# Attention scores of every block as float32 on 64x64 tiles of the matmul engine, two quads to a run

## The chip, the cores and the metric

The kernel runs on 1 core of one Trainium2 chip. The metric is the device time of one execution in microseconds (us), the median over runs.

## The reference

Sliding-window attention over 4 sequences of 576 tokens, 8 heads of 64 dimensions, window 64, and behind it two feed-forward networks without a residual path.

```python
scores = scale * np.matmul(q, k.transpose(0, 1, 3, 2))        # scale = 1/8
mask = (rel >= 0) & (rel < window)                            # rel = query - key
scores = np.where(mask, scores, -1000000000.0)
scores = scores - np.max(scores, axis=-1, keepdims=True)
attn = np.exp(scores)
attn = attn / (np.sum(attn, axis=-1, keepdims=True) + 1e-09)
return np.matmul(attn, v).astype(np.float32)
...
h = x @ w_in; r = np.maximum(h, 0.0); g = r * r               # first network, 512 -> 2048 -> 512
return (g @ w_out).astype(np.float32)
...
g = np.maximum(0.01 * h, h)                                   # second network, same sizes
```

x has 2304 rows (4 x 576) of 512 columns. The weights of both networks come as float64 and are turned into float32 on the chip.

## The kernel before, in words

**Blocks and quads.** The 2304 tokens are 18 blocks of 128 queries. A block has two quads (c = 0, 1) of four heads each. Within a block the queries are two halves (g = 0, 1) of 64, and each half sees 128 keys, its own 64 and the 64 before; a block's keys are 192 columns (KW).

**Token groups.** `BLOCKS` cuts the tokens into groups t of 512, 384, 512, 384, 512. The first network runs group by group, with 16 chunks of its 2048 hidden columns (`step`, lines 578 to 652): a chunk's 12 matmuls into bank h (line 590), ReLU, square and the split of the result on ACT and DVE, then the 12 matmuls of an earlier chunk into the four banks acc (line 636). Products of the networks are split: each float32 operand is a rounded part (type float32r) and its remainder, and three float32r matmuls stand for one product. While group t runs, attention makes the x of group t+1, so attention's matmuls stand between those of the first network until some 422 us. From 508 us on the second network runs alone (lines 820 and 909). The first group runs as 256-column halves while its weights are still being converted (DVE lines 317 to 329 and 284, ACT lines 314 and 281).

**A quad** (`quad`, lines 398 to 569) has these steps: load v; scores; mask (line 375, DVE); row maximum (507, DVE); four exponentials with row sums (510, ACT); reciprocal (516, 517) and normalising (520, DVE); four transposes (531, PE) into bank t; copy to pt (ACT); eight matmuls with v, the weighing (537, PE), into bank t; the result into x as rounded part (ACT, line 281) and remainder (DVE, line 284). The scores come in three ways:
- blocks 0 and 1 ("early") and blocks 2 to 5 ("plain", `NPLAIN=6`): q and k of both quads are loaded once for a block (`pair_load`, line 383), quad 0 on partitions 0 to 63 and quad 1 on 64 to 127. Eight float32 matmuls of 64 rows by 64 columns on 128 key columns (line 435) go into bank s (the second early quad into bank h). In the trace a float32 matmul of lines 435 and 537 is two records.
- blocks 6 to 17 (split): each quad loads q and k twice, onto both partition halves (line 459, 4 loads), ACT rounds k to kh and q to qs, DVE makes kl = k - kh and the remainder of q in the lower half of qs; eight matmuls of 128 rows by 128 columns on all 192 keys (line 485) in two groups of four, each group into bank s; each group is masked in two halves of 64 rows by 256.

Banks s and t and the SBUF tiles qr, qs, kr, kh, kl, u and pt are single buffers; v has two. Plain quads use u and kl in turn for the scores; split quads use u.

**The order of the work.** The program registers every operation with `op(engine, cost, due, fn, reads, writes)`: a cost and a due time, both written by hand. `Plan.order` (line 121) then plays the program through on the host: on each engine the ready operation with the earliest due time goes next, a slot is taken in the order of its registered turns, and a `margin` delays readiness. The order found there is fixed; on the chip each engine, and SP's queue of DMA issues, runs its list in order and waits where it must. `quads` gives every quad its time e, by which it should be done, evenly spread over the stretch in which its group must be made (`spread`, line 947). A split quad's scores are due at e - 8.0 and e - 7.2, its transposes at e - 1.6, its weighing at e - 0.4; a plain quad's scores at e - 6.5 f with f up to 1.3.

Of the kernel before, what the change touches and what calls it, by code (L numbers as in the profile page):

```python
# [41 lines left out]
    LAG=4, NPLAIN=6, NEARLY=2, SB=6, END=1.5, P0=5.2, LEAD=5.0, WF0=60.0, WF1=20.0, XC=18.0, WP=9.0, WO=8.0,  # L42
    AX=-1.0, AY=0.0, YP=1.0, FS=5.0, FMAX=1.3, EV0=0.5, EV1=1.5,
# [206 lines left out]
def build(ctx, tc, qp, kp, vp, w1, w2, caps, ident, out, prm=PRM):  # L250
# [147 lines left out]
    def quad(i, b, c, e, sp_):  # L398
        plain = b < prm["NPLAIN"]
        early = b < prm["NEARLY"]  # L400
        spare = 0.0 if plain else prm["SPARE"]
        f = min(max(sp_ / prm["FS"], 1.0), prm["FMAX"]) if plain else 1.0
        ax, ay = (0.0, prm["YP"]) if plain else (prm["AX"], prm["AY"])
        v = slot(wp, "w0", [P, 2, HQ * D], F32, NCH) if early else slot(vpool, "v", [P, 2, HQ * D], F32, 2)
        if early:
            u = slot(wp, "w1", [P, HQ, P], F32, NCH)
        elif plain and i % 2:
            u = slot(ap, "kl", [P, HQ, P])
        else:
            u = slot(ap, "u", [P, HQ, P])  # L410
        pt = slot(wp, "w0", [P, HQ, P], F32, NCH) if early else slot(ap, "pt", [P, HQ, P])
# [3 lines left out]
        if early:  # L415
            tp = slot(ps_acc, f"acc{i % 2 * 2}", [P, HQ, P])
            pv = slot(ps_acc, f"acc{i % 2 * 2 + 1}", [P, HQ // 2, P])
        else:
            tp = slot(ps_t, "t", [P, HQ, P])
            pv = slot(ps_t, "t", [P, HQ // 2, P])  # L420

        dma(
            e - min(9.0, 2 * sp_ - 0.6),
            lambda: nc.sync.dma_start(out=v.ap, in_=vp[b, c]), P * 2 * HQ * D * 4, writes=[(v, 0)],
        )
        if plain:
            q, k = pairs[b]
            st = slot(ps_h, "h", [P, HQ, P], F32, 2) if early and c else slot(ps_s, "s", [P, HQ, P])
            d = slice(c * D, (c + 1) * D)

            def scores():
                for h in range(HQ):
                    for g in range(2):
                        o = g * WIN
                        nc.tensor.matmul(
                            out=st.ap[o : o + WIN, h, :], lhsT=q.ap[d, h, o : o + WIN],
                            rhs=k.ap[d, h, o : o + P], start=True, stop=True,
                        )

            def mask():  # L440
                fst = (is_first(b, 0), is_first(b, 1))
                if fst[0] == fst[1]:
                    mask_into(u.ap, st.ap, slice(0, P), fst[0])
                else:
                    for g in range(2):
                        r = slice(g * WIN, (g + 1) * WIN)
                        mask_into(u.ap[r], st.ap[r], r, fst[g])

            op("pe", 1.1, e - 6.5 * f, scores, [(q, c), (k, c)], [(st, 0)])
            op("dve", dve_cost(512), e - 5.5 * f, mask, [(st, 0), cap], [(u, 0)])  # L450
        else:
            q = slot(ap, "qr", [P, HQ, P])
            k = slot(ap, "kr", [P, HQ, KW])
            qs = slot(ap, "qs", [P, HQ, P], F32R)
            kh = slot(ap, "kh", [P, HQ, KW], F32R)
            kl = slot(ap, "kl", [P, HQ, KW], F32R)

            def load(dst, src, g):
                nc.sync.dma_start(out=dst.ap[g * D : (g + 1) * D], in_=src[b, c])

            for g in range(2):
                dma(e + ax - 13.0, lambda g=g: load(q, qp, g), D * HQ * P * 4, writes=[(q, g)])
            for g in range(2):
                dma(e + ax - 12.9, lambda g=g: load(k, kp, g), D * HQ * KW * 4, writes=[(k, g)])
            op(
                "act", act_cost(HQ * KW), e + ax - 10.4, lambda: copy(kh.ap, k.ap),
                [(k, 0), (k, 1)], [(kh, 0)],
            )
            op(
                "dve", dve_cost(HQ * KW), e + ax - 10.0,  # L470
                lambda: sub(nc.vector, kl.ap, k.ap, kh.ap), [(k, 0), (k, 1), (kh, 0)], [(kl, 0)],
            )
            op("act", act_cost(512), e + ax - 10.0, lambda: copy(qs.ap, q.ap), [(q, 0), (q, 1)], [(qs, 0)])
            op(
                "dve", dve_cost(512), e + ax - 9.5,
                lambda: sub(nc.vector, qs.ap[D:P], q.ap[D:P], qs.ap[D:P]), [(q, 1)], [(qs, 0)],
            )
            for g in range(2):
                st = slot(ps_s, "s", [P, 2, 256])

                def scores(st=st, g=g):
                    for i2 in range(2):
                        h = 2 * g + i2
                        for m, kk in enumerate((kh, kl)):
                            nc.tensor.matmul(  # L485
                                out=st.ap[:, i2, 0:KW], lhsT=qs.ap[:, h, :], rhs=kk.ap[:, h, :],
                                start=m == 0, stop=m == 1,
                            )

                def mask(st=st, g=g, e2=0):  # L490
                    r = slice(e2 * WIN, (e2 + 1) * WIN)
                    mask_into(
                        u.ap[r, 2 * g : 2 * g + 2, :], st.ap[r, :, e2 * WIN : e2 * WIN + P],
                        r, is_first(b, e2),
                    )

                t0 = e + ax + 0.8 * g
                op("pe", 0.43, t0 - 7.0, scores, [(qs, 0), (kh, 0), (kl, 0)], [(st, 0)], margin=spare)
                for e2 in range(2):
                    op(  # L500
                        "dve", dve_cost(256), t0 - 6.2 + 0.3 * e2,
                        lambda m=mask, e2=e2: m(e2=e2), [(st, 0), cap], [(u, g, e2)],
                    )
        parts = [(u, 0)] if plain else [(u, g, e2) for g in range(2) for e2 in range(2)]
# [24 lines left out]
        def transpose():  # L529
# [3 lines left out]
        def weigh():  # L533
            for h in range(HQ):
                o = h % 2 * D
                for g in range(2):
                    nc.tensor.matmul(  # L537
                        out=pv.ap[o : o + D, h // 2, g * WIN : (g + 1) * WIN],
                        lhsT=v.ap[:, g, h * D : (h + 1) * D],
                        rhs=pt.ap[:, h, g * WIN : (g + 1) * WIN], start=True, stop=True,  # L540
                    )
# [21 lines left out]
        def part(m):  # L563
            return x.ap[:, m, kk, o : o + P]
# [512 lines left out]
```

## Time and profile before

| | us |
|---|---|
| median of 3 runs (884.1 to 886.19) | 885.02 |
| the profiled execution | 887.48 |
| its span, first to last instruction | 885.70 |
| PE busy in the span | 866.2 |
| DVE busy | 634.6 |
| ACT busy | 502.9 |

PE is the matmul engine, PEld its weight loads, which run beside the matmuls; DVE, ACT and POOL are the vector, scalar and general engines; SP issues the DMAs. A row names the line of the code, the engine, the operation and the tiles as out<-in. The starts of matmuls are measured; their ends are modelled, so busy times of neighbours overlap and a stretch is best measured from start to start. "x16" is the number of records in a merged row; a bracket at its end tells how long the engine stood idle before it and who ended that.

### The profile page before, as it was taken

How to read it: one execution, taken by the hardware profiler on the slowest of the kernel's cores; microseconds unless marked ns; L12 is line 12 of the kernel's file. 1: busy time of each engine (PE TensorE's matmuls, PEld its weight loads, DVE VectorE, ACT ScalarE, POOL GpSimd, SP SyncE). 2: the span in 40 equal slices, each digit the busy share in tenths (PEclk: the TensorE clock that was granted, in tenths of full speed). 3: DMA queues.
4: the chain of work that ended last, by engine and by line, in shares of the span. 5: the costliest groups of instructions: out<-in, count | busy, mean ns of one | idle time of the engine just before them, and what ended most of it. 6: DMA issues, size and time to landing. Idle time of an engine off the chain costs nothing.

```text
span 885.7 us, 13760 instructions
## 1 busy us (share of the span) xinstructions
PE 866.2 (98%) x5032; PEld 771.0 (87%) x5032; DVE 634.6 (72%) x1230; ACT 502.9 (57%) x1141; POOL 0.2 (0%) x4
## 2 busy tenths in 40 slices
PE   7789999999999999999999999999999999999998
PEld 6678788999888888999888899988899888999886
DVE  6989898777777787988666567695387775576540
ACT  5757776655454465655434366763377653567530
POOL 0000000000000000000000000000000000000000
PEclk8989999999999999999999999999999999999999
DMA  7665554324644436653534122331322422222201
GB/s 294 184 191 158 164 161 119 120 84 125 209 149 145 170 123 205 191 163 118 179 130 143 48 88 67 130 124 45 119 72 93 146 72 71 95 72 96 96 1 71
DMA packets 49795, 111.45 MB, mean 126 GB/s; under 512 B 6208, under 2 KB 7488, under 8 KB 49728
## 3 DMA queue, kind: packets, MB, share of 16 engines
q1 hardware_dynamic: 49728, 110.58, 39.0%
q8 instruction: 39, 0.64, 0.3%
q14 instruction: 28, 0.23, 0.1%
HBM read 92.73 MB, written 17.83 MB: 125 GB/s over the span
## 4 chain that ended last, share of the span: by engine, by line
PE 90%; DVE 5%; DMA 2%; ACT 2%; issue 1%; SPq 0%; DVEq 0%; ACTq 0%
PE h L590 21%; PE acc L636 20%; PE acc L909 15%; PE h L820 8%; PE s L820 6%; PE s L909 4%; PE t L909 4%; PE acc L820 3%; PE t L820 3%; PE s L485 2%; PE t L537 2%; PE t L531 1%; DMA wst<-w1b 1%; DVE u L375 1%; DMA wst<-w2a 1%
## 5 line engine op out<-in xcount | busy, mean ns | idle before, releaser
L590 PE MATMUL h<-x,w 128*128 128x512 f32 (+2 forms) x1008 | 225.5, 367 | 5.5 <-ACT e L610 2.7
L636 PE MATMUL acc<-g,w 128*128 128x512 f32 (+2 forms) x1008 | 222.6, 364 | 2.7 <-ACT g L281 2.7
L590 PEld LDWEIGHTS h<-x,w 128*128 128x128 f32 x1008 | 178.7, 191 | 28.4 <-ACT e L610 2.9
L636 PEld LDWEIGHTS acc<-g,w 128*128 128x128 f32 x1008 | 177.6, 191 | 23.9 <-ACT g L281 3.4
L909 PE MATMUL acc<-w,w 128*128 128x512 f32 x576 | 146.2, 389 | 0.0
L909 PEld LDWEIGHTS acc<-w,w 128*128 128x128 f32 x576 | 108.1, 188 | 22.4
L284 DVE TENSOR_TENSOR w<-wst,w 128x512 fp32r<-128x512 f32 (+1 forms) x144 | 87.2, 641 | 30.8 <-ACT w L281 30.8
L281 ACT CAST w<-wst 128x512 fp32r<-128x512 f32 (+1 forms) x144 | 78.8, 582 | 44.8 <-PE acc L909 25.2
L820 PE MATMUL h<-w,w 128*128 128x384 f32 x432 | 85.1, 334 | 0.0
L610 ACT ACTIVATE e<-h 128x512 f32<-128x512 f32 (+2 forms) x84 | 44.9, 534 | 60.8 <-PE h L590 60.2
L820 PEld LDWEIGHTS h<-w,w 128*128 128x128 f32 x432 | 75.9, 188 | 0.2
L314 ACT ACTIVATE wst<-wst 128x512 f32<-128x512 f32 x64 | 43.1, 674 | 49.4 <-DMA wst<-w1b 25.6
L375 DVE SCALAR_TENSOR_TENSOR u<-s,cap 64x256 f32<-64x256 f32 (+2 forms) x101 | 43.9, 434 | 21.0 <-PE s L485 18.0
L284 DVE TENSOR_TENSOR g<-e,g 128x512 fp32r<-128x512 f32 (+2 forms) x84 | 51.6, 614 | 8.9 <-ACT g L281 5.1
L820 PE MATMUL s<-w,w 128*128 128x384 f32 x288 | 57.9, 335 | 0.0
L619 DVE TENSOR_TENSOR e<-e 128x384 f32<-128x384 f32 (+1 forms) x64 | 39.7, 620 | 19.9 <-ACT g L618 19.6
L820 PEld LDWEIGHTS s<-w,w 128*128 128x128 f32 x288 | 50.7, 188 | 0.1
L510 ACT ACTIVATE u<-u,nm 128x128 f32<-128x128 f32 x112 | 43.6, 391 | 8.2 <-DVE nm L507 8.2
L323 DVE SCALAR_TENSOR_TENSOR e<-wst,e 128x512 int32<-128x512 int32 x64 | 44.2, 691 | 1.7
L329 DVE SCALAR_TENSOR_TENSOR e<-wst,e 128x512 int32<-128x512 int32 x64 | 44.1, 689 | 1.4
L281 ACT COPY pt<-t 128x512 f32<-128x512 f32 (+1 forms) x44 | 24.5, 556 | 36.2 <-PE t L531 31.4
L317 DVE TENSOR_SCALAR e<-wst 128x512 int32<-128x512 int32 x64 | 27.0, 421 | 20.3 <-ACT wst L314 19.3
(130 smaller groups left out, 1124.6 us busy)
## 6 DMA issues: line engine op xcount, KB each, us to landing
wst<-wf SPq DMA_DIRECT2D x96, 256.0 KB, 2.9
kr<-kp SPq DMA_DIRECT2D x48, 192.0 KB, 3.3
wst<-w1a SPq DMA_DIRECT2D x16, 512.0 KB, 3.8
wst<-w2a SPq DMA_DIRECT2D x16, 512.0 KB, 4.0
v<-vp SPq DMA_DIRECT2D x32, 256.0 KB, 2.9
wst<-w1b SPq DMA_DIRECT2D x16, 512.0 KB, 4.5
wf<-e SPq DMA_DIRECT2D x32, 256.0 KB, 2.4
wst<-w2b SPq DMA_DIRECT2D x16, 512.0 KB, 4.6
```

Source lines behind the costliest of these rows:

```text
L281: nc.scalar.copy(out=dst, in_=src)
L284: eng.tensor_tensor(out=lo, in0=src, in1=f32(hi), op=ALU.subtract)
L314: nc.scalar.activation(out=top, in_=top, func=AF.Copy, scale=2.0**-112)
L323: nc.vector.scalar_tensor_tensor(out=cv.ap, in0=words(1), scalar=-(1 << 31), in1=cv.ap, op0=ALU.bitwise_and, op1=ALU.bitwise_or,)
L329: nc.vector.scalar_tensor_tensor(out=cv.ap, in0=words(0), scalar=29, in1=cv.ap, op0=ALU.logical_shift_right, op1=ALU.bitwise_or,)
L375: nc.vector.scalar_tensor_tensor(out=u, in0=st, scalar=SCALE, in1=cap_s.ap[r, first, :].unsqueeze(1).to_broadcast([r.stop - r.start, st.sh ...
L510: nc.scalar.activation(out=u.ap[:, h, :], in_=u.ap[:, h, :], func=AF.Exp, bias=nm.ap[:, h : h + 1], scale=1.0, accum_out=sm.ap[:, h : h + 1],)
L590: nc.tensor.matmul(out=hp.ap[:, c0 : c0 + n1], lhsT=wi[:, a, kk, :], rhs=x.ap[:, b, kk, c0 : c0 + n1], start=(kk == 0 and m == 0), stop=(k ...
L610: nc.scalar.activation(out=r.ap, in_=hp.ap[:, c], func=AF.Relu)
L636: nc.tensor.matmul(out=ac[d].ap[:, c0 : c0 + n1], lhsT=wo[:, a, d * P : (d + 1) * P], rhs=g.ap[:, b, c0 : c0 + n1], start=begin, stop=end, ...
L820: nc.tensor.matmul(out=ps.ap, lhsT=view(v, i), rhs=xs[s, i][b].ap[:, u], start=begin and i == 0 and m == 0, stop=i == 1 and m == 2, skip_g ...
L909: nc.tensor.matmul(out=accs[3 * h + tt].ap, lhsT=v.ap[:, b, tt * P : (tt + 1) * P], rhs=w.ap[:, a, :], start=n == 0 and m == 0, stop=last ...
```

## The change

Blocks 0 to 3 keep `quad`, all of them with float32 scores; their tiles are u and pt in turn, and the transposed weights are copied back into the same tile. Blocks 4 to 17 (`NDUO=4`) become a `duo`: q and k of the block are loaded once; 16 float32 matmuls score both quads in one run, head by head, quad 0 into bank s and quad 1 into bank t; each quad is masked at once, quad 1 first; the two softmax chains follow, 2.2 us apart by their due times, quad 0 in u and quad 1 in pt; each quad is transposed into bank t and copied back; 16 matmuls weigh both in one run into one full bank t; one ACT copy and one DVE subtraction of 512 columns put the result into x. The scores are due at e - 12 (`DS`), the transposes at e - 5.2 and e - 3.4, the weighing at e - 1.8, with e that of the block's second quad. The split of q and k (lines 452 to 503) is gone. The planner's cost of an exponential is 0.57 us (`EXPC`) where it was 0.385, that of a score run 0.55 for a quad (1.1 before) and for a duo; the weighing of a duo has 1.1. `softmax` and `mask` hold the old steps unchanged; `load_v` is the old load.

```diff
--- before.py
+++ after.py
@@ -39,8 +39,8 @@
 NP = NCH // 2
 
 PRM = dict(
-    LAG=4, NPLAIN=6, NEARLY=2, SB=6, END=1.5, P0=5.2, LEAD=5.0, WF0=60.0, WF1=20.0, XC=18.0, WP=9.0, WO=8.0,
-    AX=-1.0, AY=0.0, YP=1.0, FS=5.0, FMAX=1.3, EV0=0.5, EV1=1.5,
+    LAG=4, NDUO=4, NEARLY=2, DS=12.0, EXPC=0.57, SB=6, END=1.5, P0=5.2, LEAD=5.0, WF0=60.0, WF1=20.0, XC=18.0, WP=9.0, WO=8.0,
+    YP=1.0, FS=5.0, FMAX=1.3, EV0=0.5, EV1=1.5,
     SPARE=0.2, NACT=0, WARM=20, WC=0.3, WD=1e6, AL=0.6, CS=0.7,
     QB=-0.5, QE=-2, QL=0.0, QT=1,
...
+    def scores(b, sts):
+
+        q, k = pairs[b]
+        for h in range(HQ):
+            for c, st in sts:
+                d = slice(c * D, (c + 1) * D)
+                for g in range(2):
+                    o = g * WIN
+                    nc.tensor.matmul(
+                        out=st.ap[o : o + WIN, h, :], lhsT=q.ap[d, h, o : o + WIN],
+                        rhs=k.ap[d, h, o : o + P], start=True, stop=True,
+                    )
...
+    def transpose(u, tp, pt, due):
+        def run():
+            for h in range(HQ):
+                nc.tensor.transpose(out=tp.ap[:, h, :], in_=u.ap[:, h, :], identity=id_s.ap)
+
+        op("pe", 0.44, due, run, [*((u, "n", h) for h in range(HQ)), idt], [(tp, 0)], margin=prm["SPARE"])
+        op("act", act_cost(512), due + 0.4, lambda: copy(pt.ap, tp.ap), [(tp, 0)], [(pt, "t")])
...
+    def weigh(v, pt, pv, k0):
+        for h in range(HQ):
+            o = h % 2 * D
+            for g in range(2):
+                nc.tensor.matmul(
+                    out=pv.ap[o : o + D, k0 + h // 2, g * WIN : (g + 1) * WIN],
+                    lhsT=v.ap[:, g, h * D : (h + 1) * D],
+                    rhs=pt.ap[:, h, g * WIN : (g + 1) * WIN], start=True, stop=True,
...
+    def to_x(b, pv, k0, k1, due):
...
+        n = (k1 - k0) * P
+        op("act", act_cost(n), due, lambda: copy(part(0), pv.ap), [(pv, 0)], hi)
+        op("dve", dve_cost(n), due + 0.3, lambda: sub(nc.vector, part(1), pv.ap, part(0)), [(pv, 0), *hi], lo)
...
+        u = slot(wp, "w1", [P, HQ, P], F32, NCH) if early else slot(ap, ("u", "pt")[i % 2], [P, HQ, P])
...
+        q, k = pairs[b]
+        st = slot(ps_h, "h", [P, HQ, P], F32, 2) if early and c else slot(ps_s, "s", [P, HQ, P])
+        op("pe", 0.55, e - 6.5 * f, lambda: scores(b, [(c, st)]), [(q, c), (k, c)], [(st, 0)])
+        op("dve", dve_cost(512), e - 5.5 * f, lambda: mask(b, u, st), [(st, 0), cap], [(u, 0)])
+        softmax(u, i < prm["NACT"], (e - 4.7 * f, e - 4.0 * f, e - 2.4 * f))
+        transpose(u, tp, u, e + ay - 1.6)
+        op("pe", 0.65, e + ay - 0.4, lambda: weigh(v, u, pv, 0), [(u, "t"), (v, 0)], [(pv, 0)])
...
+    def duo(b, e):
+
+        vs = [load_v(b, c, False, e - 12.0) for c in range(2)]
+        us = [slot(ap, ("u", "pt")[c], [P, HQ, P]) for c in range(2)]
+        sts = [slot(ps_s, "s", [P, HQ, P]), slot(ps_t, "t", [P, HQ, P])]
+        q, k = pairs[b]
+        op(
+            "pe", 0.55, e - prm["DS"], lambda: scores(b, list(enumerate(sts))),
+            [(q, 0), (q, 1), (k, 0), (k, 1)], [(st, 0) for st in sts], margin=prm["SPARE"],
         )
...
+        for c in (1, 0):
             op(
...
+                "dve", dve_cost(512), e - prm["DS"] + 1.0 + 0.1 * (1 - c),
+                lambda c=c: mask(b, us[c], sts[c]), [(sts[c], 0), cap], [(us[c], 0)],
+            )
+        for c in range(2):
+            d = 2.2 * c
+            softmax(us[c], False, (e - 9.8 + d, e - 9.0 + d, e - 6.4 + d))
+        for c in range(2):
+            transpose(us[c], slot(ps_t, "t", [P, HQ, P]), us[c], e - 5.2 + 1.8 * c)
+        pv = slot(ps_t, "t", [P, KD, P])
+
+        def run():
+            for c in range(2):
+                weigh(vs[c], us[c], pv, c * HQ // 2)
+
+        rd = [x for c in range(2) for x in ((us[c], "t"), (vs[c], 0))]
+        op("pe", 1.1, e - 1.8, run, rd, [(pv, 0)], margin=prm["SPARE"])
+        to_x(b, pv, 0, KD, e - 0.6)
...
@@ -973,14 +954,18 @@
     dma(-99.9, lambda: nc.sync.dma_start(out=cap_s.ap, in_=caps), P * 2 * P * 4, writes=[cap])
     dma(-99.8, lambda: nc.sync.dma_start(out=id_s.ap, in_=ident), P * P * 4, writes=[idt])
     pair_load(1, -99.0)
-    for b in range(2, prm["NPLAIN"]):
+    for b in range(2, NQB):
         e, _, _, gap = next(q for q in quads if q[1] == b)
-        pair_load(b, e - 6.5 * min(max(gap / prm["FS"], 1.0), prm["FMAX"]) - 6.0)
+        early = 6.5 * min(max(gap / prm["FS"], 1.0), prm["FMAX"])
+        pair_load(b, e - early - 6.0 if b < prm["NDUO"] else e + gap - prm["DS"] - 6.0)
     for k in range(2 * NCH):
         st = next(q for q in steps if q[2][0][2] == k // 2)
         weight(k, st[3] + (k % 2) * st[4] - prm["LEAD"])
     for i, (e, b, c, gap) in enumerate(quads):
-        quad(i, b, c, e, gap)
+        if b < prm["NDUO"]:
+            quad(i, b, c, e, gap)
+        elif c:
+            duo(b, e)
     for n, (t, i, parts, T, dt, wave) in enumerate(steps):
         last = n + 1 == len(steps) or steps[n + 1][0] != t
         T2 = steps[n + 1][3] + steps[n + 1][4] if n + 1 < len(steps) else t_end
```

## Rows read from the trace of the kernel before

**Rows 1.** The page's first part: each engine's busy time and share.
```profile
PE 866.2 (98%) x5032; PEld 771.0 (87%) x5032; DVE 634.6 (72%) x1230; ACT 502.9 (57%) x1141; POOL 0.2 (0%) x4
```

**Rows 2.** Table by stretches: length, busy PE, PEld, DVE, ACT, POOL, clock, DMA, GB/s.
```profile
24.00:68.00 44.00, 35.34 (x309) 31.79 (x304) 38.13 (x78) 30.00 (x91) 0.00 (x0) 0.88 0.61 188
...
121.00:425.00 304.00, 302.04 (x1939) 271.32 (x1939) 242.00 (x466) 171.78 (x435) 0.00 (x0) 1.00 0.48 148
...
508.00:885.70 377.70, 373.68 (x1884) 339.13 (x1882) 233.71 (x468) 210.83 (x418) 0.00 (x0) 1.00 0.26 86
```

**Rows 3.** Timeline of PE: start, us, engine, line, op, tiles; split scores.
```profile
321.79 2.88 PE L590 MATMUL h<-x,w 128*128 128x512 f32 x12
324.51 0.25 PE L485 MATMUL s<-kh,qs 128*128 128x192 f32 x1
...
324.93 1.56 PE L636 MATMUL acc<-g,w 128*128 128x512 f32 x6
326.33 0.25 PE L485 MATMUL s<-kh,qs 128*128 128x192 f32 x1
```

**Rows 4.** Timeline of PE: transposes, weighing and float32 scores of block 5.
```profile
100.71 0.60 PE L531 MATMUL t<-ident,u 128*128 128x128 f32 x4
101.06 1.63 PE L590 MATMUL h<-x,w 128*128 128x512 f32 x6
102.62 0.73 PE L537 MATMUL t<-pt,v 128*64 128x64 f32 x16
103.29 1.67 PE L590 MATMUL h<-x,w 128*128 128x512 f32 x6
104.80 2.91 PE L636 MATMUL acc<-g,w 128*128 128x512 f32 x12
107.63 1.09 PE L435 MATMUL s<-kh,qs 64*64 64x128 f32 x16
108.65 3.06 PE L590 MATMUL h<-x,w 128*128 128x512 f32 x12
111.55 0.62 PE L636 MATMUL acc<-g,w 128*128 128x512 f32 x2
```

**Rows 5.** Groups by line: a split score; one line: durations min/median/max of weighing.
```profile
L485 PE MATMUL s<-kh,qs 128*128 128x192 f32 x96 | 23.9, 275 | 0.5 <-DVE u L375 0.5
...
L537 PE MATMUL t<-pt,v x512: 222/222/271, 34.1 to 421.7; 128*64 128x64 f32 x171
```

**Rows 6.** Timeline of PE: two float32 quads back to back, banks s and h.
```profile
8.41 0.76 PE L435 MATMUL s<-w,w 64*64 64x128 f32 x10 [0.99 <-DVE w L375]
8.91 0.33 PE L435 MATMUL h<-w,w 64*64 64x128 f32 x2
9.00 0.28 PE L435 MATMUL s<-w,w 64*64 64x128 f32 x2
9.07 0.28 PE L435 MATMUL h<-w,w 64*64 64x128 f32 x2
9.11 0.28 PE L435 MATMUL s<-w,w 64*64 64x128 f32 x2
...
9.93 0.38 PE L967 MATMUL t<-w 128*128 128x128 f32 x1
```

**Rows 7.** Waits of PE from 68 to 508 us: total, times, longest.
```profile
PE t L531 <- DVE u L520: 0.6, 1, 0.6
PE s L485 <- DVE u L375: 0.5, 2, 0.3
```

**Rows 8.** Groups by line: the subtraction that makes kl, count, busy, mean ns.
```profile
L284 DVE TENSOR_TENSOR kl<-kr,kh 128x768 fp32r<-128x768 f32 x24 | 22.8, 950 | 0.6 <-PE t L531 0.6
```

**Rows 9.** SP's timeline, the chain that ended last, PE's timeline, near 55 us.
```profile
52.88 1.18 SPq L459 DMA_DIRECT2D qr<-qp  x2
...
55.45 5.53 DMA wst<-w2a
...
61.98 1.79 PE L590 MATMUL h<-x,w 128*128 128x256 f32 x9 [2.66 <-ACT e L610]
```

More of the change, by code (lines that the diff above doesn't have):

```diff
@@ L396, in pair_load, with mask, softmax @@
         dma(due + 0.01, lambda: load(k, kp), P * HQ * KW * 4, writes=[(k, 0), (k, 1)])
[L398 to L408, printed above, removed]
-        else:
-            u = slot(ap, "u", [P, HQ, P])
-        pt = slot(wp, "w0", [P, HQ, P], F32, NCH) if early else slot(ap, "pt", [P, HQ, P])
+    def scores(b, sts):
[9 more added lines that the diff above has]
+                    )
+    def mask(b, u, st):
+        fst = (is_first(b, 0), is_first(b, 1))
+        if fst[0] == fst[1]:
+            mask_into(u.ap, st.ap, slice(0, P), fst[0])
+        else:
+            for g in range(2):
+                r = slice(g * WIN, (g + 1) * WIN)
+                mask_into(u.ap[r], st.ap[r], r, fst[g])
+    def softmax(u, act_norm, due):
         nm = slot(sp, "nm", [P, HQ], F32, 3)
@@ L414, in quad @@
         rc = slot(sp, "rc", [P, HQ], F32, 3)
[L415 to L503, printed above, removed]
@@ L504, in quad @@
-        parts = [(u, 0)] if plain else [(u, g, e2) for g in range(2) for e2 in range(2)]
         def reduce_max():
@@ L527, in norm_head @@
             )
-        def transpose():
+        op("dve", dve_cost(512), due[0], reduce_max, [(u, 0)], [(nm, 0)])
+        for h in range(HQ):
+            op("act", prm["EXPC"], due[1], lambda h=h: exp(h), [(nm, 0), (u, 0)], [(u, "x", h), (sm, h)])
+        ex = [(u, "x", h) for h in range(HQ)]
+        op("dve", 0.25, due[2], recip, [(sm, h) for h in range(HQ)], [(rc, 0)])
+        if act_norm:
+            for h in range(HQ):
+                op("act", 0.2, due[2] + 0.2, lambda h=h: norm_head(h), [(rc, 0), (u, "x", h)], [(u, "n", h)])
+        else:
+            op("dve", dve_cost(512), due[2] + 0.2, norm, [(rc, 0), *ex], [(u, "n", h) for h in range(HQ)])
@@ L560, in quad @@
         o = b * P - starts[t]
[L561 removed]
         def part(m):
[L564 to L569 removed]
+            return x.ap[:, m, k0:k1, o : o + P]
@@ new lines, in to_x, with load_v @@
+        hi = [(x, 0, kk, b) for kk in range(k0, k1)]
+        lo = [(x, 1, kk, b) for kk in range(k0, k1)]
+        n = (k1 - k0) * P
+        op("act", act_cost(n), due, lambda: copy(part(0), pv.ap), [(pv, 0)], hi)
+        op("dve", dve_cost(n), due + 0.3, lambda: sub(nc.vector, part(1), pv.ap, part(0)), [(pv, 0), *hi], lo)
+    def load_v(b, c, early, due):
+        v = slot(wp, "w0", [P, 2, HQ * D], F32, NCH) if early else slot(vpool, "v", [P, 2, HQ * D], F32, 2)
+        dma(
+            due, lambda: nc.sync.dma_start(out=v.ap, in_=vp[b, c]), P * 2 * HQ * D * 4, writes=[(v, 0)],
+        )
+        return v
```

42 lines of the change are left out of this document (16 added, 26 removed).

## The prediction

> **What bounds the kernel now.** I read the page's busy line first: the matmul engine (PE) is busy for 98% of the span [rows 1]. That only says where to look, so the table by stretches came next [rows 2]. There the reader is to see three things. From 121 to 425 us, where blocks 6 to 17 are scored and weighed, PE is busy 302.04 of 304.00 us at a granted clock of 1.00, and DVE 242 of 304: PE's own work sets the time there, and DVE and ACT work that goes is worth only the waits that it ends. From 24 to 68 us PE is idle for 44.00 - 35.34 = 8.7 us, its clock is 0.88, and DVE is busy 38.13 of 44 us: there the work on weights and attention holds PE up. From 508 us on no attention is left; nothing of the change reaches that stretch except by its start.
>
> So the change is priced as PE time between fixed neighbours. In the timeline of PE, an instruction group's price is the start of the next group less its own start. Twelve undisturbed 512-column matmuls take 324.51 - 321.79 = 2.72 us, six 1.36 [rows 3]; what a neighbour takes above this is the price of going into or out of the group beside it.
>
> **PE, old pieces.** From rows 3 and 4:
> - one group of 4 split scores: 324.93 - 324.51 = 0.42, and the six matmuls behind it 326.33 - 324.93 = 1.40, so 0.04 on leaving: 0.46. A quad has two: 0.92. The 96 records of L485 with kh [rows 5] and as many with kl are 24 quads of 8, blocks 6 to 17;
> - four transposes: 0.35;
> - the six matmuls between transposes and weighing: 1.56, so 0.20 (I put half to each);
> - 8 weighing matmuls (16 records): 0.67 with rounding, taken as 0.66; leaving: 1.51 - 1.36 = 0.15;
> - 8 float32 64x64 scores of one quad (16 records): 1.02; entering 2.83 - 2.72 = 0.11, leaving 2.90 - 2.72 = 0.18: 1.31.
>
> Transposes and weighing together are 0.35 + 0.20 + 0.66 + 0.15 = 1.36 a quad. A block of two quads costs 2 x (0.92 + 1.36) = 4.56 with split scores, and 2 x (1.31 + 1.36) = 5.34 for blocks 4 and 5, which are float32 already but quad by quad.
>
> **PE, the new scores.** A duo's 16 matmuls are 32 records. The trace has no such run, but it has the nearest thing: in the first blocks the float32 scores of quad 0 (into bank s, contraction rows 0 to 63) and of quad 1 (into bank h, rows 64 to 127) stand back to back [rows 6]. The reader is to see that while both are there, 2 records of s and 2 of h start every 0.11 us (9.00, 9.07, 9.11), where s alone starts 2 in that time (16 in 1.02 us is 0.11 a pair, with the ends). The two row halves run side by side and neither slows the other. The duo alternates the halves head by head, into s and t, so its lower end is 8 steps of 0.11 with the same ends: 1.02 for both quads. The upper end is no overlap, twice the run: 2.04. Between lies the order of rows 6, all of one quad first: 9.93 - 8.41 = 1.52. I take 1.02, since alternating heads feeds both halves from the start; with 0.11 and 0.18 that is 1.31 a block. The Trainium skill ("TensorE: Matmul & The Clock Gate", Part 3, The mechanism) says that matmuls start and end strictly in program order. The trace differs: h's first two records start at 8.91, before s's last at 9.00 and later, although s stands first in the program. By that rule the duo would need one step of 0.11 more, some 1.5 us over 14 blocks.
>
> **PE, the new weighing.** One run of 32 records. In the old run of 16 the starts span 0.73 - 0.22 (one record [rows 5]) = 0.51, 0.034 a step; 16 more add 0.54: 0.66 + 0.54 = 1.20, with one entry (0.10) and one exit (0.15) 1.45. Upper end: 2 x 0.66 + 0.25 = 1.57.
>
> **Sum on PE.** New block: 1.31 + 2 x (0.35 + 0.10) + 1.45 = 3.66. Blocks 6 to 17: 12 x (4.56 - 3.66) = 10.8. Blocks 4 and 5: 2 x (5.34 - 3.66) = 3.4. Together **14.2 us** off the bound. Blocks 0 to 3 keep their PE work.
>
> **Waits of PE after 68 us.** They are few: 304.00 - 302.04 = 2.0 us up to 425 us [rows 2]. The 0.5 us of split scores that waited for the mask to free bank s goes, as a duo has two banks. The transposes' 0.6 us behind the normalising stays [rows 7].
>
> **Off PE, costed at nothing.** Per split quad go an ACT copy of k and of q, two DVE subtractions (the one of k 0.95 us [rows 8]) and four half-size masks, for which one full mask comes (two where only one half block is first of its sequence); a block's two x copies become one each on ACT and DVE. PE, busy 99% there, hides all of it; uncovered it could only gain. On SP a split quad's 4 loads of q and k become 2 a block. The copy of the transposes into u instead of pt adds no instruction. What it adds is a wait: the next block's masks need the weighing of this block done, and v's two buffers are both held by one duo, so SP's wait for them stands ahead of weight loads. Block spacing by the due times is 16 to 29 us against DS=12, so I price these waits at nothing, upper end in the rivals.
>
> **The stretch from 24 to 68 us.** PE's chain stands on a weight load that lands after 5.53 us, and PE idles 2.66 us for it; SP issued it behind the four q and k loads of block 6, the first of them at 52.88 us, right after block 4's scores had freed their tile [rows 9]. These become 2 loads, and stand behind a later scoring (block 4's duo is due 0.4 us after e of its first quad, not 8.4 before). Block 4's DVE work moves later too, out of a stretch where DVE is 87% busy. Bounds: worse by as much again (-2.7) to all 8.7 us of idle time gone. I take the 2.7 us of this one wait, the nearest row.
>
> **The forecast.** 14.2 + 0.5 + 2.7 = 17.4 us. The profiled execution took 887.5 us (885.7 span and 1.8 around it), so 870.1; the median of the runs is 885.0, 2.5 below it, so **867.6**.
>
> **Rivals.**
> 1. *The row halves don't run side by side* in this order. Scores 2.04: a block costs 4.68, so twelve lose 0.12 each (1.4) and two gain 0.66 each (1.3), nothing on PE; with the two smaller terms 885.0 - 3.2 + 0.1 = 881.9. Against it: rows 6. The Trainium skill (the same page, Part 2, Back-to-back issue gap) gives some 81 ns for each load and matmul of 128 columns in a sustained stream; an estimate by it is 32 x 0.081 = 2.6 us of scores a block, which would make the kernel some 5 us slower than before. The trace doesn't agree: 16 in 1.02 us are 64 ns, and half of that where two quads overlap. Chance 0.05.
> 2. *SP's queue blocks the weights.* The two v loads and the pair load of a duo wait for a weighing or a scoring that the planner believes done, and a weight load behind them comes late, as in rows 9, once or twice more: 2 x 2.7 lost, not 2.7 won, 885.0 - 14.7 + 5.4 = 875.7. For: that is how the present stall arose. Against: fewer loads than before. Chance 0.08.
> 3. *PE waits for the duo's chain* (slower). Place: bank t holds scores, two transposes and the result one after the other, and u is mask, weights and transpose in one; between scoring and weighing lie the masks, eight exponentials, normalising and two copies. If the planner has it end too early, PE stands before the transposes and again before the weighing. From 14.7 / 14 = 1.05 us of waiting a block on it decides; at 2 us a block it is 28 us: 885.0 - 14.7 + 28 = 898.3. For: scores are entered at 0.55 us and take 1.31. Against: PE itself is late by that, so what waits behind it in order is late too, and the exponentials are entered at 0.57, not 0.385. In the old chain PE waited 0.6 us once. Chance 0.05.
> 4. *The matmuls are not what the diff says* and nothing moves: 885. The 64*64 form is in the trace [rows 4], so 0.02.
>
> **The numbers.** Forecast 0.80. Low end: 14.2 + 0.5 + 8.7 gives 861.6. High end of the forecast's own terms: scores at 1.52 (14 x 0.50 = 7.0) and weighing at its upper end (1.7), no early gain: 885.0 - 14.7 + 8.7 = 879.0. The range 862 to 879 holds rival 2 as well; rivals 1, 3 and 4 and some tails lie outside. A measurement can tell about 0.2%, 1.8 us, from no change: faster is the forecast, rival 2 and most of rival 1 (0.91), same 0.04, slower 0.05.
>
> **What would show it.** The timeline of a duo: 32 score records of s and t mixed, some 1.0 us to the next group (rival 1: 2.0), and 32 weighing records in 1.2 us. PE's wait list after 68 us: still 2 us or less, with no transposes behind normalising or weighing behind a copy beyond 0.1 us a block (rival 3). The stretch to 68 us: PE idle 6 us, and no weight load landing after 5 us behind q and k (rival 2). The end of the first network's last matmul, 508 us now, some 17 us sooner, and from there on the same 378 us. The prediction fails if PE's idle time grows over the sum, or if that last stretch changes by more than 1 us.

## The result, and the profile after

The changed kernel took 872.37 us (median of four runs, one of which, of 4784.8 us, was disturbed and is left out of the ratio) where the kernel before, on the same chip, took 885.05: a ratio of 0.985 with an interval of 0.983 to 0.987. The forecast was 867.6 with a range of 862 to 879. Two repeats gave 0.983 (0.982 to 0.985) and 0.985 (0.983 to 0.988). The profiled executions stand further apart than the medians: 887.48 and 871.45, spans 885.70 and 869.66, so 16.0 us.

The page's first part, after; it answers to [rows 1]:

```profile
PE 849.9 (98%) x5224; PEld 755.1 (87%) x5224; DVE 574.8 (66%) x1100; ACT 469.5 (54%) x1079; POOL 0.2 (0%) x4
```

PE lost 16.3 us of busy time, the span 16.0. DVE lost 59.8 and ACT 33.4, and PE is as full as before: 98%. Its idle time in the whole span is 19.8 us where it was 19.5, so what was won is PE's own work. That is how it looks when one engine's work sets the time and its neighbours only follow.

The table by stretches, after, in the columns of [rows 2]:

```profile
24.00:68.00 44.00, 33.56 (x339) 30.37 (x339) 40.33 (x82) 32.71 (x92) 0.00 (x0) 0.92 0.57 195
...
121.00:425.00 304.00, 303.12 (x2165) 269.67 (x2165) 193.77 (x356) 147.26 (x392) 0.00 (x0) 1.00 0.39 131
```

From 121 to 425 us PE is idle for 0.9 us where it was 2.0. DVE's load there fell from 242 to 194 us, and PE ran at clock 1.00 both times. In the first stretch PE was to become less idle. It is idle for 44.00 - 33.56 = 10.4 us where it was 8.7, and DVE is busier (40.33, before 38.13).

The waits of PE from 68 to 508 us are now one; they answer to [rows 7]:

```profile
PE h L571 <- DVE w L284: 0.8, 1, 0.8
```

No transpose waits for a normalising and no weighing for a copy: from 68 us on the duo's chain never holds PE up.

The timeline of PE through one duo, after (start, us, engine, line, operation, tiles; a merged row ends with its number of records):

```profile
95.73 2.88 PE L617 MATMUL acc<-g,w 128*128 128x512 f32 x12
98.54 0.33 PE L406 MATMUL s<-kh,qs 64*64 64x128 f32 x2
98.55 0.33 PE L406 MATMUL t<-kh,qs 64*64 64x128 f32 x2
98.70 0.28 PE L406 MATMUL s<-kh,qs 64*64 64x128 f32 x2
98.71 0.28 PE L406 MATMUL t<-kh,qs 64*64 64x128 f32 x2
98.81 0.28 PE L406 MATMUL s<-kh,qs 64*64 64x128 f32 x2
98.82 0.28 PE L406 MATMUL t<-kh,qs 64*64 64x128 f32 x2
...
99.57 3.06 PE L571 MATMUL h<-x,w 128*128 128x512 f32 x12
102.47 2.88 PE L617 MATMUL acc<-g,w 128*128 128x512 f32 x12
105.19 2.88 PE L571 MATMUL h<-x,w 128*128 128x512 f32 x12
107.91 0.60 PE L463 MATMUL t<-ident,u 128*128 128x128 f32 x4
108.27 3.00 PE L617 MATMUL acc<-g,w 128*128 128x512 f32 x12
111.10 0.60 PE L463 MATMUL t<-ident,pt 128*128 128x128 f32 x4
111.45 2.33 PE L571 MATMUL h<-x,w 128*128 128x512 f32 x9
113.72 0.73 PE L472 MATMUL t<-u,v 128*64 128x64 f32 x16
114.23 0.69 PE L472 MATMUL t<-pt,v 128*64 128x64 f32 x16
114.85 0.98 PE L571 MATMUL h<-x,w 128*128 128x512 f32 x3
```

Read starts, not durations. The scores take 99.57 - 98.54 = 1.03 us for both quads; one quad alone took 1.02 [rows 4]. From 98.70 on, two records of s and two of t start every 0.11 us, each pair of t 0.01 us behind its pair of s. Entering costs 98.54 - 95.73 - 2.72 = 0.09 and leaving 102.47 - 99.57 - 2.72 = 0.18. The weighing takes 114.85 - 113.72 = 1.13. All 13 score runs from here on take 1.03. Block 4's, at 59.79 us, took 1.47: its records of t began 0.44 us behind those of s.

**A ledger of PE.** Take the stretch from the 97th matmul of the first network's first product (where the 512-column groups begin) to the first matmul of the second network, and add up every attention group from its start to the next group's start. Network matmuls are set at 226.7, 173.4 and 120.0 ns each by width, as they run undisturbed; what they take above that is "borders and waits".

| us | before | after |
|---|---|---|
| the stretch | 437.05 | 421.56 |
| network matmuls | 371.29 | 371.29 |
| scores | 23.93 | 13.44 |
| transposes | 9.98 | 9.99 |
| weighing | 18.89 | 15.81 |
| borders and waits | 12.96 | 11.04 |

Scores before were 48 split groups (21.89) and block 5's two float32 quads (2.04); after they are 13 runs. The stretch gives 15.5 us: 10.5 from scores, 3.1 from weighing, 1.9 from borders and waits. What lies outside it hardly moved. The second network to the end took 377.89 and 377.92 us. The stretch began at 70.76 before and at 70.18 after: 0.6 us.

### The profile page after: what moved, and what is told of

Read it like the earlier page. It is cut to its first block, busy times and chain, and to the rows that moved or that the text cites. A ratio compares the mean times of both kernels' runs of the same rounds, so it can differ in the third digit from the quotient of the medians.

```text
span 869.7 us, 13819 instructions
## 1 busy us (share of the span) xinstructions
PE 849.9 (98%) x5224; PEld 755.1 (87%) x5224; DVE 574.8 (66%) x1100; ACT 469.5 (54%) x1079; POOL 0.2 (0%) x4
## 4 chain that ended last, share of the span: by engine, by line
PE 92%; DVE 4%; DMA 2%; ACT 2%; issue 0%; DVEq 0%; SPq 0%
PE acc L617 21%; PE h L571 21%; PE acc L890 15%; PE h L801 9%; PE s L801 6%; PE s L890 4%; PE t L890 4%; PE acc L801 3%; PE t L801 3%; PE t L472 2%; PE s L406 2%; PE t L463 2%; DMA wst<-w2a 1%; PE t L948 1%; DVE e L323 1%; DMA wst<-w1a 1%
## 5 line engine op out<-in xcount | busy, mean ns | idle before, releaser
L571 PE MATMUL h<-x,w 128*128 128x512 f32 (+2 forms) x1008 | 219.3, 363 | 3.5 <-DVE w L284 1.9
L640 DVE COPY e<-acc 128x512 f32<-128x512 f32 (+1 forms) x19 | 12.6, 664 | 49.3 <-PE acc L890 27.8
L890 PE MATMUL s<-w,w 128*128 128x512 f32 x144 | 40.5, 389 | 0.0
L890 PE MATMUL t<-w,w 128*128 128x512 f32 x144 | 40.4, 389 | 0.0
L284 DVE TENSOR_TENSOR w<-x,w 128x384 fp32r<-128x384 f32 x54 | 29.5, 553 | 13.9 <-ACT w L281 13.9
```

What stands on the lines that cost most here:

```text
L284: eng.tensor_tensor(out=lo, in0=src, in1=f32(hi), op=ALU.subtract)
L571: nc.tensor.matmul(out=hp.ap[:, c0 : c0 + n1], lhsT=wi[:, a, kk, :], rhs=x.ap[:, b, kk, c0 : c0 + n1], start=(kk == 0 and m == 0), stop=(k ...
L890: nc.tensor.matmul(out=accs[3 * h + tt].ap, lhsT=v.ap[:, b, tt * P : (tt + 1) * P], rhs=w.ap[:, a, :], start=n == 0 and m == 0, stop=last ...
```

## The experiments

The texts on record call the theories by letters. In short: by **A** the gain is PE's own list, priced from start to start (in the first two texts A says something else, that single executions spread and mostly before 70 us); by **E** a part of it comes from the work that DVE, ACT and the DMAs lost; by **G** the loads of q and k hold up weight loads in the early stretch; by **I** the planner's new costs move the early start. The kernel before ran beside every experiment, the changed kernel beside some of them; where it didn't, a difference of two medians is one between chips, and the ledger's stretch, which repeats within 0.6 us, tells more.

### Both kernels again

Nothing is edited.

> The kernel before again, nothing edited, for a second trace of it. Theory A (the spread lies in the first 70 us): 884 to 886 us as timed, and the stretch from the 97th matmul of the first network to the start of the second takes 437.1 us as in the first trace, within 0.5. Theory B (it lies elsewhere): that stretch is shorter by 2 us or more.

> The changed kernel again, nothing edited. The two profiled executions differ by 16.0 us (887.5 and 871.5), the medians by 12.7. Theory A: the difference is the spread of single executions, most of it made before 70 us (the 26 warm-up records at the start took 4.84 us in one trace and 5.92 in the other). Then the median is 871 to 874 us, 11 to 14 us under the kernel before, and in a second trace the stretch from the 97th matmul of the first network to the start of the second again differs from the old trace by 15.5 us within 0.5. Theory B: the PE saving itself varies from run to run. Then that stretch moves by 2 us or more.

> The changed kernel once more, nothing edited, beside the next one on the same chip: 871 to 872.5 us, 0.983 to 0.985 of the kernel before, in its third trace the same weight load behind block 5's q and k after 5.4 us and PE idle 10 us from 24 to 68 us.

Before: 886.08 us, stretch 436.52. After: 871.18 and 871.94, stretches 421.23 and 421.35. So the ledger's stretch repeats within 0.6 us, and the two kernels differ there by 15.0 to 15.8 us in every pairing of the traces. The medians differ by 15.1 us (871.18 against 886.29 beside it) and 13.1 (871.94 against 885.02), where 12.7 came the first time; 11 to 14 had been expected. The place where it begins doesn't repeat: 70.76 and 70.04 before, 70.18, 70.02 and 70.93 after. The early gain of 0.6 us is within that. Single runs of the kernel before went from 883.7 to 890.5 (35 runs on one chip), so a difference of some 2 us between two single executions tells nothing.

### One quad after the other in the run

```diff
-        for h in range(HQ):
-            for c, st in sts:
-                d = slice(c * D, (c + 1) * D)
+        for c, st in sts:
+            d = slice(c * D, (c + 1) * D)
+            for h in range(HQ):
```

The same 16 matmuls, in another order; nothing else differs on any engine.

> The changed kernel with one edit: within a duo's score run all eight matmuls of quad 0 come before all eight of quad 1, where they alternated head by head. PE's list differs in that alone, the other engines' lists not at all. Theory A (the two row halves overlap as far as the order lets them): the run takes some 1.5 us to the next group in place of 1.03, as the early quads showed, so 14 x 0.49 = 6.9 us more than the changed kernel, 879 us. Theory C (the halves always run side by side, whatever the order): no change, 872. Theory D (the order does not matter because they share the bus and the gain has another cause): 872 with the run at 1.03.

It took 878.05, 6.9 more than the changed kernel beside it; 0.991 (0.989 to 0.993) of the kernel before. The timeline of PE:

```profile
98.54 0.76 PE L406 MATMUL s<-kh,qs 64*64 64x128 f32 x10
99.04 0.33 PE L406 MATMUL t<-kh,qs 64*64 64x128 f32 x2
99.14 0.28 PE L406 MATMUL s<-kh,qs 64*64 64x128 f32 x2
99.20 0.28 PE L406 MATMUL t<-kh,qs 64*64 64x128 f32 x2
...
99.42 0.71 PE L406 MATMUL t<-kh,qs 64*64 64x128 f32 x10
100.06 0.74 PE L571 MATMUL h<-x,w 128*128 128x512 f32 x2
```

Here s runs alone at first, then both, then t alone: 100.06 - 98.54 = 1.52, the pattern and the price of [rows 6]. Thirteen runs are 19.77 us, 6.3 more, and the stretch is 428.03, 6.8 more. So 6.3 of the 10.5 us that the scores gain hang on the order of two loops: with alternating heads both row halves of the array work from the first record to the last.

The prediction set a rule of the Trainium skill ("TensorE: Matmul & The Clock Gate", Part 3, The mechanism) against the trace: matmuls start strictly in program order. This run differs from it as the kernel before did, for all of s stands ahead of t in the program, and t's first pair starts at 99.04, before the pairs of s at 99.14 and later. Nor does the estimate of 2.6 us hold that the prediction worked out from the same page of the Trainium skill, Part 2 (Back-to-back issue gap): the run costs 1.03 with the halves alternating and 1.52 without.

### All blocks float32, quad by quad

```diff
-    LAG=4, NPLAIN=6, NEARLY=2, SB=6, END=1.5, P0=5.2, LEAD=5.0, WF0=60.0, WF1=20.0, XC=18.0, WP=9.0, WO=8.0,
+    LAG=4, NPLAIN=18, NEARLY=2, SB=6, END=1.5, P0=5.2, LEAD=5.0, WF0=60.0, WF1=20.0, XC=18.0, WP=9.0, WO=8.0,
```

This is the kernel before without its split: DVE, ACT and the DMAs lose what they lose in the change, but the quads stay apart.

> The kernel before with float32 64x64 scores for all 18 blocks (NPLAIN=18), quad by quad and weighed quad by quad: no split of q and k, but no joint runs. DVE, ACT and the DMA queue lose the same work as in the changed kernel. Theory A (PE's time between neighbours decides): 12 blocks cost 5.34 in place of 4.56 us, so 9.4 us slower than before, 894 us, 1 or 2 us less if waits on DVE go. Theory E (the gain of the change is the work that left DVE, ACT and SP): faster than before, 875 to 883.

It took 889.74, 1.004 (1.002 to 1.005) of the kernel before: slower, with DVE at 579.9 us (changed kernel 574.8) and ACT at 471.1 (469.5). The page's first part of this kernel:

```profile
PE 871.6 (98%) x5224; PEld 767.6 (87%) x5224; DVE 579.9 (65%) x1114; ACT 471.1 (53%) x1093; POOL 0.2 (0%) x4
```

PE's busy time rose from 866.2 [rows 1] to 871.6. E falls, for nearly all the relief of DVE and ACT is here, the kernel is no faster, and in the ledger borders and waits didn't shrink (13.63, before 12.96). A had the sign and missed the size: 3.4 us where 9.4 were expected; the ledger's stretch, 440.74, is 3.7 longer. Its timeline of PE shows why:

```profile
209.87 1.09 PE L435 MATMUL s<-kr,qr 64*64 64x128 f32 x16
210.89 0.66 PE L531 MATMUL t<-ident,kl 128*128 128x128 f32 x4
211.31 1.82 PE L590 MATMUL h<-x,w 128*128 128x384 f32 x9
```

The scores stand right ahead of transposes: those take 211.31 - 210.89 = 0.42 instead of 0.35, and the scores pay no border of 0.18 on leaving. Of the 26 score runs in the ledger's stretch, 16 have an attention group right behind them. A border is paid for a visit to attention, not for a group.

### The two score runs apart

```diff
-        op(
-            "pe", 0.55, e - prm["DS"], lambda: scores(b, list(enumerate(sts))),
-            [(q, 0), (q, 1), (k, 0), (k, 1)], [(st, 0) for st in sts], margin=prm["SPARE"],
-        )
-        for c in (1, 0):
+        for c in range(2):
             op(
-                "dve", dve_cost(512), e - prm["DS"] + 1.0 + 0.1 * (1 - c),
+                "pe", 0.55, e - prm["DS"] + 2.8 * c, lambda c=c: scores(b, [(c, sts[c])]),
+                [(q, c), (k, c)], [(sts[c], 0)], margin=prm["SPARE"],
+            )
+        for c in range(2):
+            op(
+                "dve", dve_cost(512), e - prm["DS"] + 1.0 + 2.8 * c,
```

> The changed kernel with the score run undone alone: two operations of eight matmuls, due 2.8 us apart, each masked when it is there; the joint weighing stays. Theory A (the two halves share one run and one pair of borders): each block pays a second run of 1.02 and a second pair of borders of 0.27, so 14 x 1.28 = 17.9 us more than the changed kernel, some 889 us; 3.8 less if the planner sets the second run right beside another attention group everywhere, as it did in 14 of 26 runs of the all-float32 kernel. Theory F (the joint run saves nothing but waits): under 875.

It took 885.68, 0.998 (0.996 to 1.000) of the kernel before: nearly all of the gain is gone, 14.5 us against the changed kernel of another chip, 13.3 in the ledger's stretch (434.83). The timeline of PE through one quad's run, between network matmuls on both sides:

```profile
99.53 2.88 PE L572 MATMUL h<-x,w 128*128 128x512 f32 x12
102.34 1.09 PE L406 MATMUL t<-kh,qs 64*64 64x128 f32 x16
103.36 2.83 PE L618 MATMUL acc<-g,w 128*128 128x512 f32 x11
```

One quad alone takes 1.02, as in [rows 4]. In the ledger the scores are 25.52 us for 25 runs (12.1 more than in the changed kernel), borders and waits 12.29 (1.3 more, where 0.27 for each extra run had been expected). So 12 of the 13.3 us are the side-by-side running itself, and little of it is fewer borders.

### The two weighings apart

```diff
-        op("pe", 1.1, e - 1.8, run, rd, [(pv, 0)], margin=prm["SPARE"])
-        to_x(b, pv, 0, KD, e - 0.6)
+        for c in range(2):
+            op(
+                "pe", 0.55, e - 1.8 + 1.2 * c, lambda c=c: weigh(vs[c], us[c], pv, c * HQ // 2),
+                [(us[c], "t"), (vs[c], 0)], [(pv, 0)], margin=prm["SPARE"],
+            )
+        to_x(b, pv, 0, KD, e + 0.2)
```

> The changed kernel with the weighing run undone alone: two operations of eight matmuls, due 1.2 us apart; the joint scores stay; the result goes into x 0.8 us later. Theory A: 2 x 0.66 in place of 1.13 is 0.19, and a second pair of borders is 0.25, so 14 x 0.44 = 6.2 us more, 877 us, 1 more if the last block of a group comes late for the next. If the planner leaves both runs side by side, no change.

It took 877.50, 6.3 more than the changed kernel of another chip; 0.989 (0.988 to 0.991) of the kernel before. The ledger's stretch is 426.93, 5.4 more. The timeline of PE:

```profile
113.06 0.73 PE L472 MATMUL t<-u,v 128*64 128x64 f32 x16
113.73 1.65 PE L570 MATMUL h<-x,w 128*128 128x512 f32 x6
115.31 0.73 PE L472 MATMUL t<-pt,v 128*64 128x64 f32 x16
115.97 3.03 PE L616 MATMUL acc<-g,w 128*128 128x512 f32 x12
```

Twice some 0.67 with six matmuls between that take 1.58 instead of 1.36. The ledger has weighing at 18.55 (2.7 more) and borders and waits at 13.66 (2.6 more). Here, unlike with the scores, the border is half of the gain.

### The transposes in one run

```diff
-        for c in range(2):
-            transpose(us[c], slot(ps_t, "t", [P, HQ, P]), us[c], e - 5.2 + 1.8 * c)
+        tps = [slot(ps_t, "t", [P, HQ, P]), slot(ps_s, "s", [P, HQ, P])]
...
+        op("pe", 0.8, e - 3.4, turn, rd, [(tp, 0) for tp in tps], margin=prm["SPARE"])
...
-            duo(b, e)
+            duo(b, e - 0.5)
```

`turn` issues the eight transposes; ACT copies one bank back and DVE the other.

> The changed kernel with a block's eight transposes in one run, quad 0 into bank t and quad 1 into bank s, copied back by ACT and by DVE; the duo's due times 0.5 us earlier. Theory A (a visit to attention costs its borders, and two visits made one save one of them): the border between the two transposes, 1.42 us over 14 blocks, goes, and the run takes 0.71 in place of 2 x 0.355: 1.4 us under the changed kernel, some 870 us. Theory K (PE now waits for the later quad's normalising before both): no gain or a loss, with a wait of the transposes on DVE in PE's list.

It took 870.37, 0.983 (0.981 to 0.985) of the kernel before. The stretch is 420.43, 0.8 to 1.1 less than the changed kernel's three. The border of 1.42 us between the two groups has gone, but the transposes take more, 11.08 instead of 9.99, which leaves 0.3; the rest is other borders and waits. No transpose waits for DVE there. The timeline of PE shows 0.44 for the first four and 0.36 for the second:

```profile
110.39 0.60 PE L545 MATMUL t<-ident,u 128*128 128x128 f32 x4
110.83 0.60 PE L545 MATMUL s<-ident,pt 128*128 128x128 f32 x4
111.19 2.31 PE L583 MATMUL h<-x,w 128*128 128x512 f32 x9
```

The ledger sees this gain; the measured times, 870.37 and 871.18 (intervals 0.981 to 0.985 and 0.982 to 0.985), don't tell the two kernels apart.

### The early stretch: loads, and the planner's costs

The weight load that was to come in time still comes late. SP's timeline after, and one row of the chain of work that ended last, of the same kernel:

```profile
41.44 0.33 SPq L393 DMA_DIRECT2D qs<-qp  x1
41.81 1.14 SPq L393 DMA_DIRECT2D kh<-kp  x1
...
43.55 0.36 SPq L305 DMA_DIRECT2D wst<-w2a  x1
44.19 0.33 SPq L305 DMA_DIRECT2D wst<-w1a  x1
```

```profile
44.19 5.45 DMA wst<-w1a
```

These are block 5's q and k. They are scored at 98.54 us and loaded at 41.44, since their tiles are free and the list lets them go; the weight behind them lands after 5.45 us, as it did behind block 6's loads in [rows 9]. The kernel before had these loads in the same place:

```profile
41.47 0.33 SPq L393 DMA_DIRECT2D qs<-qp  x1
...
43.48 0.37 SPq L305 DMA_DIRECT2D wst<-w2a  x1
```

In the changed kernel two waits of PE stand behind the two weights. The timelines of ACT and of PE, after:

```profile
48.36 0.68 ACT L314 ACTIVATE wst<-wst 128x512 f32<-128x512 f32 x1 [3.58 <-DMA wst<-w2a]
48.94 0.57 ACT L281 COPY u<-t 128x512 f32<-128x512 f32 x1
49.66 0.69 ACT L314 ACTIVATE wst<-wst 128x512 f32<-128x512 f32 x1 [0.15 <-DMA wst<-w1a]
```

```profile
49.56 0.73 PE L472 MATMUL t<-u,v 128*64 128x64 f32 x16 [1.70 <-ACT u L281]
53.21 0.80 PE L617 MATMUL acc<-g,w 128*128 128x256 f32 x2 [2.92 <-ACT g L281]
```

ACT runs its list in order. It stands 3.58 us for the first weight; the copy that block 3's weighing needs comes behind it, and the g that the network needs comes behind the second weight. In the kernel before ACT waited there too, but block 4's scores and a weighing kept PE at work:

```profile
48.09 0.69 ACT L314 ACTIVATE wst<-wst 128x512 f32<-128x512 f32 x1 [3.06 <-DMA wst<-w2a]
```

```profile
49.16 1.09 PE L435 MATMUL s<-kr,qr 64*64 64x128 f32 x16
```

The experiment makes the loads of blocks 4 to 17 wait until a weight due 4 us earlier has been made ready:

```diff
-    def pair_load(b, due):
+    def pair_load(b, due, after=()):
...
+            k = max(k for k in range(2 * NCH) if begun[k] <= due - 4.0)
+            pair_load(b, due, [(wt[divmod(k, 2)], 1)])
```

It was run twice, the second time on one chip with the changed kernel's third run.

> The changed kernel with one wait added: the q and k loads of blocks 4 to 17 go out only when the weight that is due 4 us before them is ready; in the changed kernel block 5's go out at 41.4 us, 57 us before their scores, ahead of two weight loads, one of which lands after 5.5 us with PE idle behind it. Theory G (the early stretch's gain did not come since another pair of q and k loads stands in the same place): PE's idle time from 24 to 68 us falls from 10 to 7 us or less, 868 us or so. Theory H (the weight loads there are held by their buffers or DVE, not by q and k): no change, 871, within 1.

> The kernel with the later q and k loads once more, on the same chip as the changed kernel. If the 1.5 us that it gained against the changed kernel of another batch are the loads' (theory G), it is 1 to 3 us under the changed kernel here too, and PE's idle time from 24 to 68 us is again some 7 us in place of 10. If they were the chip's, it is within 0.7 us of it.

The first time it took 869.67 (0.980, 0.979 to 0.982), the second 871.22 (0.985, 0.982 to 0.987) beside the changed kernel's 871.94. The rows of the weight load in the chain and of 24 to 68 us in the table by stretches: first run,

```profile
43.45 4.43 DMA wst<-w1a
```

```profile
24.00:68.00 44.00, 36.69 (x345) 33.57 (x344) 40.96 (x84) 33.30 (x96) 0.00 (x0) 0.88 0.53 171
```

second run,

```profile
44.27 4.53 DMA wst<-w1a
```

```profile
24.00:68.00 44.00, 33.88 (x341) 30.81 (x340) 40.27 (x82) 32.74 (x92) 0.00 (x0) 0.92 0.56 173
```

and the changed kernel's third run, beside the second:

```profile
43.43 7.31 DMA wst<-w1a
```

The load lands sooner both times (4.4 and 4.5 us against 5.4 and 7.3), and PE's wait of 1.70 before the weighing is gone. But PE is idle for 7.3 us in the first and 10.1 in the second, where the changed kernel's three traces have 10.4, 10.3 and 10.9, and the 0.7 us between the two medians of the second is within what can be told. The traces show where the gain goes (us from the span's start):

| | weight lands | PE's wait for g ends | 512-column groups begin |
|---|---|---|---|
| changed kernel, three traces | 49.64, 49.42, 50.74 | 53.21, 53.02, 54.31 | 70.18, 70.02, 70.93 |
| loads later, two traces | 47.88, 48.80 | 51.59, 52.37 | 68.23, 70.15 |

PE goes on 3.6 to 3.7 us after the landing in all five: this wait stands behind the load. From there to the 512-column groups it is 16.6 to 17.0 us in four of them and 17.8 in the second run with later loads, which gives back 1.2 of the 1.9 us that it had won on the changed kernel's third trace. G is right about the load and about this wait; that the load sets the time of the whole stretch is not shown. What took the 17.8 us stays open.

The planner's costs:

```diff
-        op("pe", 0.55, e - 6.5 * f, lambda: scores(b, [(c, st)]), [(q, c), (k, c)], [(st, 0)])
+        op("pe", 1.1, e - 6.5 * f, lambda: scores(b, [(c, st)]), [(q, c), (k, c)], [(st, 0)])
...
-        softmax(u, i < prm["NACT"], (e - 4.7 * f, e - 4.0 * f, e - 2.4 * f))
+        softmax(u, i < prm["NACT"], (e - 4.7 * f, e - 4.0 * f, e - 2.4 * f), 0.385)
```

> The changed kernel with the planner's old costs for blocks 0 to 3 alone (score run 1.1, exponential 0.385); the code that runs is the same, in another order. The first network started at 26.5 us in both traces of the changed kernel and at 24.3 and 25.1 in those of the kernel before. Theory I (the new costs order block 2's masks and exponentials ahead of block 1's result): the first network starts 1 to 2 us sooner, 870 us. Theory J (the start is held by the loads and the warm-up's clock): no change, 871, within 1.

It took 872.42 (0.984, 0.982 to 0.985). Its first network started at 25.22 us, the changed kernel's at 26.55 and 26.57, but its stretch began at 71.06: the earlier start was given back. The ledger's stretch is 423.12, 1.6 to 1.9 longer, with 1.5 us of waits of PE for weights' remainders on DVE where the changed kernel has 0.5 to 0.8. And the changed kernel itself started at 24.96 in its third trace. So I is not shown.

Both edits, loads and transposes, in one kernel:

> The one run of transposes and the later q and k loads together. If both savings are what they seem (1.4 us of borders, some 2 us of the early stretch) they add up: 867 to 868.5 us, 0.978 of the kernel before. If they overlap, 869 to 870.

It took 870.08 (0.982, 0.980 to 0.983): not the sum of two gains. The first run of the later loads (0.979 to 0.982) hardly meets the changed kernel's intervals of other chips (0.982 to 0.985 and higher), but its repeat beside the changed kernel lies among them. No version here is shown to beat the changed kernel.

## Why the prediction was right, and where it was off

**The bound.** Right: PE's own time decides from 68 us on. The two kernels that undo PE's sharing lose 13.3 and 5.4 us of the ledger's stretch with DVE and ACT as busy as in the changed kernel (575 to 576 and 470 us), and the one that only takes the work from DVE and ACT gains nothing.

**The scores.** Forecast 1.02 for both quads, 1.03 measured over 13 runs (block 4's, before them, took 1.47); entering and leaving 0.11 and 0.18, measured 0.09 and 0.18. Rival 1, no side-by-side running, is excluded by the timeline, and the price between the bounds, 1.52, came out exactly when the loops were turned round.

**The sum on PE.** Block 4's scores lie before the ledger's stretch, and so do 1.3 of the 14.7 us; for the stretch the forecast was 13.4, and 15.5 were measured. The old attention was dearer by 1.0 than priced. A split group stands alone 32 times of 48 and takes 0.425 there, as [rows 3] gave it; the other 16 stand right beside a weighing or transposes and take 0.45 to 0.54 on average, by neighbour, but share a border with them. Together the old groups took 2.3 more and the old borders and waits 1.3 less than the prediction's terms. The new attention was cheaper by 1.1: 1.0 of it is the weighing, which the prediction extrapolated to 1.20 and which takes 1.13.

**The waits.** The duo's long chain was costed at nothing, and PE's waits after 68 us fell to 0.8 us, one wait for a weight's remainder on DVE. Rival 3 fell.

**The early stretch is the step that failed.** The 2.7 us, and block 4's 1.3, were to come there; 0.6 came in the first pair of traces, and over five traces nothing that stands out of their spread. Counted from the first network's first matmul, the way to the 512-column groups was 46.5 and 44.9 us before and 43.6, 43.5 and 46.0 after, which doesn't settle it either. The step said that four loads of block 6 ahead of the weight become two and stand behind a later scoring. That is so: they go out at 61.37 us, and PE's wait of 2.66 us is gone. But what the row shows is not block 6's alone. A pair's loads go out once the tiles of q and k come free, however late they are needed, and stand before weights. Block 5's do so at 41.47 us before and at 41.44 after, 57 us ahead of its scores. In the kernel before PE had block 4's scores to run while ACT waited for those weights; the edit moves these scores from 49.16 to 59.79 us, and PE stands for 1.70 and 2.92 us instead. I read the row as one event that the edit removes, and not as a habit of the list that the edit keeps, and booked block 4's later work as relief only. That the moved scores are the cause is read from the two timelines and was not tested. Rival 2, a weight late behind the loads once more, came about in part: the 2.7 us weren't won. Nor was time lost beyond that.

**From the profile to the median.** In profiled time the forecast was 870.1 and 871.45 came: 1.3 off, the 3.4 that the early stretch failed to give less the 2.1 that the later one gave more. The miss in the medians is larger, 872.4 against 867.6. It holds the 2.5 us that I took off because the profiled execution of before lay that much above its median. That is not a constant of the measurement: the profiled execution of after lies 0.9 us below its median, and single runs of one kernel spread over 6.8 us. Had both distances been set to nothing, the forecast would have been 870.1.

## What to carry to other kernels

Price a small matmul group from its start to the next group's start, with the border into and out of its neighbours apart, take the mean over all such groups, standing alone and side by side, and count a border per visit to that kind of work: groups that stand together share it. Where matmuls use half the rows of the array, alternate the halves in the program, matmul by matmul: 1.03 us for two quads here, 1.52 one after the other in one run, twice 1.02 in two. Before a stall is booked as won, look for what will stand in the same place after the edit, and don't explain a microsecond from two single traces before the spread of runs is known.

## What was not expected of the hardware

- On 64x64 tiles four records (two of s, two of t) start within 0.11 us with both row halves at work, where one half alone starts two; a run of 32 costs 1.03 us and one of 16 costs 1.02.
- A border is charged between the network's matmuls and attention's, and hardly between attention's own: transposes right behind float32 scores cost 0.06 us more than their 0.35 (mean of 14), where the way back to the network's matmuls costs 0.18.
- Eight transposes into two banks in one run cost 0.79 us, two groups of four apart 0.357 each: of the 0.10 of border between them that was saved, 0.08 came back inside the run.
- The same list of 26 small matmuls at the start, which the edit doesn't touch, took 4.84 and 5.71 us in the two traces of before and 5.92, 5.92 and 4.52 in the three of after; the first network started at 24.27 and 25.13 us in the two traces of before, and at 24.96 to 26.57 in the three of after.
